# Linear attention plus a gated MLP on one core: scaling of q moved to ACT and POOL, states per unit, and the last three chunks transposed by DMA

## The chip, the cores and the metric

The kernel runs on one core of a Trainium2 chip. The metric is the device time of one execution in microseconds. A timed execution is about 2.1 us longer than the span from the first to the last instruction that a profile shows. The kernel before takes 250.9 to 251.2 us in its first timed runs.

Engine names: PE multiplies matrices, PEld is its weight load, DVE, ACT and POOL do elementwise work, SP issues most DMAs.

## The reference

Per batch and head, attention with a decay `lam` runs over blocks; its output, with the heads side by side, is the input `x` of a two-layer network.

```python
for b in range(nb):                       # blocks of the sequence
    intra = (qb @ kb.T * Dmask) @ vb      # inside the block, with decay
    inter = (qb * lam_pow) @ kv_state     # what earlier blocks left
    out[block] = intra + inter
    kv_state = lam_block * kv_state + (kb * rev_pow).T @ vb
h = x @ w_in                              # 3072 x 512 @ 512 x 2048
g = h * erf(softplus(h))
y = g @ w_out                             # 2048 x 512
```

Inputs are q, k, v of 4 x 8 x 768 x 64 in fp32; the result is 3072 x 512.

## The kernel before

The work is cut into 16 units (batch, half of the sequence, four heads) and 8 chunks of 384 tokens, two units each. A unit is loaded, q and k are scaled by powers of the decay (`scale_q`, `scale_k`), both are transposed (`alpha`), the scores are made (`beta`), then the states (`states`), then the attention output (`outputs`), which ACT copies into `xT`. A chunk then has 16 up-projection steps (`up_proj`), four gate steps, and 12 down-projection steps. The program is written out period by period: period `c` holds the up-projections of chunk `c`, the gates of chunk `c-1`, the down-projections of chunk `c-2` and, put in at numbered positions, the attention of the chunk that comes next.

```python
def scale_q(self):                                   # DVE
    ...
        nc.vector.tensor_scalar(out=self.qd[...], in0=qs[:, hh], scalar1=qpow[:, h:h + 1], ...)
def scale_k(self):                                   # POOL
    ...
        nc.gpsimd.tensor_scalar(out=self.kd[...], in0=ks[:, hh], scalar1=kpow[:, h:h + 1], ...)
def alpha(self):                                     # 12 PE transposes, 2 copies out of PSUM
    ps = pa.tile([128, 2, 8, 128], BF16, name="qk_ps", tag="a")
    ...
            nc.tensor.transpose(out=ps[:, pr, n, :], in_=self.qd[:, pr, n], identity=ident[:])
            nc.tensor.transpose(out=ps[:, pr, HB + n, :], in_=self.kd[:, pr, n], identity=ident[:])
...
def up_proj(c, ko):
    ...                                              # 4 matmuls of 384 columns into h_ps (2 buffers)
    nc.vector.tensor_copy(h[:, ko % GRP, :], ps[:, 0:T])
    if ko % GRP == GRP - 1:
        e = es[c, g] = mw.tile([128, GRP, T], FP32, name="e_sb", tag="e", bufs=5)
        nc.scalar.activation(out=e[:], in_=h[:], func=Af.Softplus)
def gate(c, g, dve=()):
    nc.scalar.activation(out=e[:], in_=e[:], func=Af.Erf)
    for j in range(GRP):                             # on POOL, in the last period on DVE
        eng.tensor_mul(gs[c][:, g * GRP + j, :], h[:, j, :], e[:, j, :])
def down_proj(c, i):                                 # 4 of 16 matmuls of 512 columns into y_ps (2 buffers)
    ...
    if part == 3:
        nc.scalar.copy(y[:], ps[:])                  # ACT, then a store by SP
...
for fn in pool:                                      # pool: k and v scaling, then the gates
    put(0, fn)
...
pts = {0: (8, 12, 10, 14, 15, 16), 1: (5, 11, 8, 13, 15, 16), ...}   # alpha, alpha, beta, beta, states, outputs
```

Of the kernel before, what the change touches and what calls it, by code (L numbers as in the profile page):

```python
# [12 lines left out]
BF16 = mybir.dt.bfloat16  # L13
# [7 lines left out]
def kernel(  # L21
# [19 lines left out]
    KI, KO = DM // 128, DF // 128  # L41
    GRP = 4
# [72 lines left out]
    load(1, "k", nc.scalar)  # L115
    load(1, "q")
# [19 lines left out]
    class Unit:  # L136
# [5 lines left out]
        def scale_q(self):  # L142
            qs = staged[self.i][0]
            self.qd = aw.tile([128, 2, HB, 2, D], BF16, name="qd", tag="qd", bufs=4)
            for hh in range(4):
                h = 4 * self.pp + hh
                nc.vector.tensor_scalar(out=self.qd[:, hh // 2, :, hh % 2, :], in0=qs[:, hh],  # L147
                                        scalar1=qpow[:, h:h + 1], scalar2=None, op0=Alu.mult)

        def scale_k(self):  # L150
            ks = staged[self.i][1]
            self.kd = aw.tile([128, 2, HB, 2, D], BF16, name="kd", tag="kd", bufs=4)
            for hh in range(4):
                h = 4 * self.pp + hh
                nc.gpsimd.tensor_scalar(out=self.kd[:, hh // 2, :, hh % 2, :], in0=ks[:, hh],  # L155
                                        scalar1=kpow[:, h:h + 1], scalar2=1.0,
                                        op0=Alu.mult, op1=Alu.mult)
# [12 lines left out]
        def alpha(self):  # L170

            ps = pa.tile([128, 2, 8, 128], BF16, name="qk_ps", tag="a")
            self.qk = aw.tile([128, 2, 2, HB, 128], BF16, name="qk_sb", tag="qk")
            for pr in range(2):
                for n in range(HB):
                    nc.tensor.transpose(out=ps[:, pr, n, :], in_=self.qd[:, pr, n], identity=ident[:])  # L176
                    nc.tensor.transpose(out=ps[:, pr, HB + n, :], in_=self.kd[:, pr, n], identity=ident[:])  # L177
            for pr in range(2):
                copy = nc.scalar.copy if self.i < 4 and pr else nc.vector.tensor_copy
                copy(self.qk[:, pr].rearrange("p a n i -> p (a n) i"), ps[:, pr, 0:2 * HB, :])  # L180

        def beta(self):

            self.sc = aw.tile([128, 2, 2, HB, 128], BF16, name="sc_sb", tag="sc")
            for pr in range(2):
                ps = pa.tile([128, 2, 4, 128], FP32, name="sc_ps", tag="a")
                for n in range(HB):
                    for hh in range(2):
                        r = slice(64 * hh, 64 * hh + 64)
                        nc.tensor.matmul(ps[:, hh, n, :], lhsT=self.qk[r, pr, 1, n, :],  # L190
                                         rhs=self.qk[r, pr, 0, n, :])
                h0 = 4 * self.pp + 2 * pr
                m = mask[:, h0:h0 + 2, :]
                m = bass.AP(tensor=m.tensor, offset=m.offset, ap=[m.ap[0], m.ap[1], [0, HB], m.ap[2]])
                nc.vector.tensor_mul(self.sc[:, pr], ps[:, :, 0:HB, :], m)  # L195
# [4 lines left out]
    def states(c):  # L200

        ps = pa.tile([128, 2, 8, D], FP32, name="dk_ps", tag="a")
        us = units[2 * c:2 * c + 2]
# [25 lines left out]
    def outputs(c):  # L229
# [4 lines left out]
        first = set()  # L234

        def start(*key):
            new = key not in first
            first.add(key)
            return new

        for u, ps in zip(us, pss):
            for n in range(HB):
# [3 lines left out]
                for pr, hh in ((0, 0), (1, 1), (1, 0), (0, 1)):  # L246
                    r = slice(64 * hh, 64 * hh + 64)
                    nc.tensor.matmul(ps[r, pr, n, :], lhsT=u.kv[r, pr, g, :], rhs=u.qk[r, pr, 0, n, :],  # L248
                                     start=start(u.pp, pr, hh), stop=False, skip_group_check=True)
        for u, ps in zip(us, pss):  # L250
            for pr in range(2):
                for n in range(HB):
                    for hh in range(2):
                        r = slice(64 * hh, 64 * hh + 64)
                        nc.tensor.matmul(ps[r, pr, n, :], lhsT=u.vb[:, pr, n, hh, :],  # L255
                                         rhs=u.sc[:, pr, hh, n, :],
                                         start=start(u.pp, pr, hh), stop=True, skip_group_check=True)
# [6 lines left out]
    def up_proj(c, ko):  # L264
# [10 lines left out]
        if c == 0 and ko % 2:  # L275
# [34 lines left out]
    def slots(c):  # L310

        a, b = units[2 * c:2 * c + 2]
        return [a.alpha, b.alpha, a.beta, b.beta, lambda: states(c), lambda: outputs(c)]

    a, b = units[0:2]
    a.scale_q()
    a.scale_k()
    a.alpha()
    late_consts()
    load(3)  # L320
    a.beta()
# [8 lines left out]
    b.alpha()  # L330
    b.beta()
    states(0)
# [9 lines left out]
    for c in range(NCH + 2):  # L342
# [23 lines left out]
        elif c == 1:  # L366
            pool = kv(u) + gates[:1] + kv(u + 1) + gates[1:2] + [lambda: [load_wout(g) for g in range(4)]] + gates[2:]
        elif c == 2:
            pool = gates[:2] + kv(u, u + 1) + gates[2:]
        elif c == 3:  # L370
            pool = kv(u, u + 1) + gates
            put(21, units[u + 2].scale_kv)
            put(25, units[u + 3].scale_kv)
# [4 lines left out]
        for pos, w in {0: ((6, u), (11, u + 1)), 1: ((3, u), (9, u + 1)), 2: ((15, u), (19, u + 1)),  # L378
                       3: ((3, u), (6, u + 1), (21, u + 2), (25, u + 3))}.get(
                           c, ((8, u + 2), (13, u + 3))):  # L380
            if w < len(units):
                put(pos, units[w].scale_q)
                put(pos, load, w + 3)
        if c + 1 < NCH:
            pts = {0: (8, 12, 10, 14, 15, 16), 1: (5, 11, 8, 13, 15, 16), 2: (17, 21, 19, 23, 25, 27),
# [39 lines left out]
```

## Time and profile before

| | us |
|---|---|
| timed, first runs | 250.91 (250.9 to 251.16) |
| span of the execution that was profiled first | 252.3 |
| up to the first matmul of the third chunk | 69.75 |
| from there to the first down-projection matmul | 14.34 |
| from there to the end | 168.21 |

The lines of the next block are from the table of stretches of the kernel before, with rows left out. Each has: stretch, its length, then busy time and number of instructions of PE, PEld, DVE, ACT and POOL, the granted tensor clock as a share of full speed, the busy share of the DMA engines, and GB/s.

```profile
0.00:69.00 69.00, 44.89 (x464) 26.39 (x465) 42.87 (x110) 33.82 (x36) 36.16 (x67) 1.00 0.91 178
69.00:84.00 15.00, 14.00 (x64) 7.03 (x64) 8.16 (x15) 13.91 (x12) 13.01 (x19) 0.78 0.96 175
...
105.00:130.00 25.00, 23.97 (x223) 13.91 (x226) 19.37 (x48) 17.30 (x16) 24.16 (x38) 1.00 0.73 172
130.00:219.00 89.00, 87.98 (x721) 49.23 (x731) 56.09 (x125) 62.21 (x55) 64.19 (x76) 1.00 0.20 60
```

Up to 69 us PE is busy for 44.89 us only, while DMA moves 178 GB/s. From 130 to 219 us PE is busy for 87.98 of 89 us. Between the two lies a stretch at a mean clock of 0.78. The view of who waited for whom, limited to PE and to 84 to 222 us, gives the sum, the number of waits and the longest:

```profile
PE h_ps L272 <- DVE h_sb L278: 1.3, 2, 0.8
```

So in that stretch PE is the limit, with 1.3 us of waits for another engine. The "restart" is the first up-projection matmul of the third chunk, after PE has stood idle. The chain of work that ended last shows what holds it at 69.75 us (start, duration, engine, tile, line):

```profile
61.39 2.24 POOL wout_sb L133 x3
63.62 3.88 POOL gT L290 x4
67.52 1.48 ACT e_sb L281
69.00 0.70 ACT xT L258
69.75 6.32 PE h_ps L272 x20
```

POOL's issue of the w_out loads and then its gates of the first chunk come first. A softplus on ACT (L281) waits for a gate to free its `e` buffer. The `xT` copy (L258) stands behind that softplus, and the up-projection needs it.

### The profile page before, as it was taken

How to read it: one execution, taken by the hardware profiler on the slowest of the kernel's cores; microseconds unless marked ns; L12 is line 12 of the kernel's file. 1: busy time of each engine (PE TensorE's matmuls, PEld its weight loads, DVE VectorE, ACT ScalarE, POOL GpSimd, SP SyncE). 2: the span in 40 equal slices, each digit the busy share in tenths (PEclk: the TensorE clock that was granted, in tenths of full speed). 3: DMA queues.
4: the chain of work that ended last, by engine and by line, in shares of the span. 5: the costliest groups of instructions: out<-in, count | busy, mean ns of one | idle time of the engine just before them, and what ended most of it. 6: DMA issues, size and time to landing. Idle time of an engine off the chain costs nothing.

```text
span 252.3 us, 4777 instructions
## 1 busy us (share of the span) xinstructions
PE 218.2 (86%) x1770; PEld 119.5 (47%) x1792; DVE 150.6 (60%) x350; ACT 146.6 (58%) x136; POOL 155.9 (62%) x225
## 2 busy tenths in 40 slices
PE   0347978888499999999899999999999999996993
PEld 0225444445245545555465556555655555542441
DVE  1655468499537873879669936993577344418300
ACT  4022475895299242794399249924993499569010
POOL 2275034099969996299999993991199219930000
PEclk9999999999959999999999999999999999999799
DMA  6979998777998377578577701020101010210212
GB/s 139 212 162 197 197 203 180 171 162 146 193 196 176 79 174 174 157 179 229 132 178 177 211 3 42 0 86 0 45 0 68 18 42 3 83 42 1 102 67 83
DMA packets 84647, 29.68 MB, mean 118 GB/s; under 512 B 77456, under 2 KB 81552, under 8 KB 84624
## 3 DMA queue, kind: packets, MB, share of 16 engines
q1 hardware_dynamic: 77200, 24.40, 39.9%
q0 software_dynamic: 4224, 4.19, 10.2%
q10 hardware_dynamic: 3200, 0.79, 1.5%
q8 instruction: 14, 0.23, 0.4%
q14 instruction: 9, 0.07, 0.1%
HBM read 27.27 MB, written 6.29 MB: 133 GB/s over the span
## 4 chain that ended last, share of the span: by engine, by line
PE 69%; DVE 13%; POOL 5%; DMA 4%; ACT 4%; issue 3%; SPq 1%; DVEq 0%; ACTq 0%; POOLq 0%
PE y_ps L301 31%; PE h_ps L272 28%; DVE h_sb L278 3%; POOL gT L290 3%; DVE qd L147 3%; DMA k_st<-in_k_dram 3%; DVE sc_sb L195 3%; DVE kv L225 2%; PE sc_ps L190 2%; PE o_ps L255 2%; PE o_ps L248 2%; PE qk_ps L176 2%; PE qk_ps L177 1%; ACT xT L258 1%; ACT e_sb L287 1%
## 5 line engine op out<-in xcount | busy, mean ns | idle before, releaser
L290 POOL TENSOR_TENSOR gT<-h_sb,e_sb 128x384 bf16<-128x384 f32 x112 | 107.9, 1011 | 38.6 <-ACT e_sb L287 31.5
L272 PE MATMUL h_ps<-xT,win_sb 128*128 128x384 bf16 x512 | 102.8, 336 | 7.9 <-DVE h_sb L278 4.3
L278 DVE COPY h_sb<-h_ps 128x384 f32<-128x384 f32 x120 | 65.4, 554 | 58.9 <-PE h_ps L272 50.6
L301 PE MATMUL y_ps<-wout_sb,gT 128*128 128x512 bf16 x362 | 92.1, 385 | 3.6 <-ACT y_sb L305 2.3
L272 PEld LDWEIGHTS <-win_sb 128*128 128x128 bf16 x512 | 49.6, 100 | 50.2 <-issue 16.5
L281 ACT ACTIVATE e_sb<-h_sb 128x1536 f32<-128x1536 f32 x32 | 47.3, 1483 | 33.9 <-DVE h_sb L278 20.8
L301 PEld LDWEIGHTS <-gT 128*128 128x128 bf16 x384 | 37.1, 99 | 40.9 <-issue 4.8
L287 ACT ACTIVATE e_sb<-e_sb 128x1536 f32<-128x1536 f32 x32 | 44.8, 1472 | 0.1
L155 POOL TENSOR_SCALAR kd<-k_st,pows 128x192 bf16<-128x192 f32 x64 | 26.5, 442 | 19.4 <-DMA k_st<-in_k_dram 15.3
L195 DVE TENSOR_TENSOR sc_sb<-sc_ps,mask 128x768 bf16<-128x768 f32 x32 | 29.2, 950 | 5.2 <-PE sc_ps L190 5.1
L305 ACT COPY y_sb<-y_ps 128x512 f32<-128x512 f32 x24 | 13.8, 577 | 28.7 <-PE y_ps L301 26.0
L176 PE MATMUL qk_ps<-ident,qd 128*128 128x128 bf16 x96 | 14.3, 231 | 9.7 <-DVE qd L147 9.2
L147 DVE TENSOR_SCALAR qd<-q_st,pows 128x192 bf16<-128x192 f32 x64 | 21.9, 404 | 1.1 <-ACT pows L101 1.0
L258 ACT CAST xT<-o_ps 128x768 bf16<-128x768 f32 x16 | 12.0, 800 | 17.9 <-PE o_ps L255 17.9
L163 POOL CAST vb<-v_st 128x384 bf16<-128x384 f32 x32 | 15.7, 522 | 8.1 <-DMA v_st<-in_v_dram 8.0
L180 DVE COPY qk_sb<-qk_ps 128x768 bf16<-128x768 bf16 x28 | 14.5, 552 | 8.9 <-PE qk_ps L177 8.4
L176 PEld LDWEIGHTS <-qd 128*128 128x128 bf16 x96 | 9.6, 102 | 12.9 <-DVE qd L147 11.9
L190 PE MATMUL sc_ps<-qk_sb 64*128 64x128 bf16 x192 | 9.5, 228 | 6.0 <-ACT qk_sb L180 4.7
L177 PE MATMUL qk_ps<-ident,kd 128*128 128x128 bf16 x96 | 14.1, 230 | 0.0
L225 DVE SCALAR_TENSOR_TENSOR kv<-kv,lamblk,dk_ps 128x64 bf16<-128x64 bf16 x64 | 12.9, 275 | 1.4 <-PE dk_ps L214 1.4
L190 PEld LDWEIGHTS <-qk_sb 64*128 64x128 bf16 x192 | 5.7, 97 | 12.2 <-ACT qk_sb L180 5.4
L248 PE MATMUL o_ps<-qk_sb,kv 64*64 64x128 bf16 x160 | 8.6, 229 | 2.5 <-DVE kv L225 1.9
(37 smaller groups left out, 88.1 us busy)
## 6 DMA issues: line engine op xcount, KB each, us to landing
q_st<-in_q_dram SPq DMA_DIRECT2D x64, 96.0 KB, 2.6
v_st<-in_v_dram SPq DMA_DIRECT2D x64, 96.0 KB, 2.6
out_dram<-y_sb SPq DMA_DIRECT2D x24, 256.0 KB, 2.0
k_st<-in_k_dram SPq DMA_DIRECT2D x56, 96.0 KB, 2.5
win_sb<-in_moe_w_in_dram POOLq DMA_DIRECT2D x4, 512.0 KB, 10.1
wout_sb<-in_moe_w_out_dram POOLq DMA_DIRECT2D x4, 512.0 KB, 10.5
k_st<-in_k_dram ACTq DMA_DIRECT2D x8, 96.0 KB, 3.6
lam_bc<-in_lam_dram SPq DMA_DIRECT2D x1, 4.0 KB, 2.8
```

The source lines that it names most:

```text
L147: nc.vector.tensor_scalar(out=self.qd[:, hh // 2, :, hh % 2, :], in0=qs[:, hh], scalar1=qpow[:, h:h + 1], scalar2=None, op0=Alu.mult)
L155: nc.gpsimd.tensor_scalar(out=self.kd[:, hh // 2, :, hh % 2, :], in0=ks[:, hh], scalar1=kpow[:, h:h + 1], scalar2=1.0, op0=Alu.mult, op1=A ...
L176: nc.tensor.transpose(out=ps[:, pr, n, :], in_=self.qd[:, pr, n], identity=ident[:])
L190: nc.tensor.matmul(ps[:, hh, n, :], lhsT=self.qk[r, pr, 1, n, :], rhs=self.qk[r, pr, 0, n, :])
L195: nc.vector.tensor_mul(self.sc[:, pr], ps[:, :, 0:HB, :], m)
L225: nc.vector.scalar_tensor_tensor(out=u.kv[:, pr, g + 1, :], in0=u.kv[:, pr, g, :], scalar=lamblk[:, hp:hp + 1], in1=dk, op0=Alu.mult, op1= ...
L272: nc.tensor.matmul(ps[:, 0:T], lhsT=win_sb[:, kc, ko * 128:(ko + 1) * 128], rhs=xT[:, kc, :], start=(kc == 0), stop=(kc == KI - 1))
L278: nc.vector.tensor_copy(h[:, ko % GRP, :], ps[:, 0:T])
L281: nc.scalar.activation(out=e[:], in_=h[:], func=Af.Softplus)
L287: nc.scalar.activation(out=e[:], in_=e[:], func=Af.Erf)
L290: eng.tensor_mul(gs[c][:, g * GRP + j, :], h[:, j, :], e[:, j, :])
L301: nc.tensor.matmul(ps[:], lhsT=gs[c][:, ko, t * 128:(t + 1) * 128], rhs=wout_sb[:, ko, :], start=(ko == 0), stop=(ko == KO - 1))
```

## The change

Its intent: take DVE off the critical start by scaling q of units 0 to 3 on ACT and of units 4 and 5 on POOL; make the states unit by unit; issue the intra part of the outputs before the inter part, which needs the states; and take 72 of the 192 transposes off PE by letting the DMA engines transpose the last six units. For units 10 and 11 the DMA needs k early, so their k scaling moves from POOL, where it came late, to DVE. All 12 DMA transposes stand in SP's queue. The diff below is shortened: square brackets stand for calls, and not shown are the new order of the first two units, the layout of the transposed tile, and the buffers of `qd` (3 for 4) and of that tile (3).

```diff
-    load(1, "k", nc.scalar)
-    load(1, "q")
+    load(1, "qk")
...
+                if self.i < 4:
+                    nc.scalar.mul(self.qd[...], qs[:, hh], qpow[:, h:h + 1])
+                elif self.i < 6:
+                    nc.gpsimd.tensor_scalar(out=self.qd[...], in0=qs[:, hh], ...)
+                else: ...                                     # DVE, as before
+                eng = nc.vector if self.i in (10, 11) else nc.gpsimd       # scale_k
...
+        def flip(self):                                      # FIRST_X = 10
+            if self.i < FIRST_X:
+                return
+            self.qk = aw.tile([128, 2, 2, HB, 128], BF16, name="qk_sb", tag="qk", bufs=3)
+            for a, src in enumerate((self.qd, self.kd)):
+                nc.sync.dma_start_transpose(self.qk[:, a]..., src[:]...)
...                                      # outputs: intra of both units first, then inter
-        if c == 0 and ko % 2:
+        if c == 0 and ko % 2 or c == 1 and ko in (9, 11, 13, 15):          # h copies on ACT
...
         elif c == 1:
-            pool = kv(u) + gates[:1] + kv(u + 1) + gates[1:2] + [w_out loads] + gates[2:]
+            pool = [x.scale_k, x.scale_q, x.cast_v, load, y.scale_k, y.scale_q, y.cast_v, load] + gates[:2]
+            pool += [w_out loads] + gates[2:]
...
         elif c == 3:
-            put(21, units[u + 2].scale_kv); put(25, units[u + 3].scale_kv)  # q at 21, 25 too
+            for w, pos in ((u + 2, 12), (u + 3, 17)):
+                put(pos, units[w].scale_k); put(pos, units[w].scale_q)
+                put(pos + 2, units[w].flip); put(pos + 3, units[w].cast_v); put(pos + 3, load, w + 3)
...
+        for w in (2 * c + 4, 2 * c + 5):
+            if c > 3 and w < len(units):
+                put(26, units[w].flip)
-        1: (5, 11, 8, 13, 15, 16)
+        1: (3, 9, 5, 11, 13, 16)
```

More of the change, by code (lines that the diff above doesn't have):

```diff
@@ L41 @@
     KI, KO = DM // 128, DF // 128
+    FIRST_X = 10
     GRP = 4
@@ L143, in scale_q @@
             qs = staged[self.i][0]
-            self.qd = aw.tile([128, 2, HB, 2, D], BF16, name="qd", tag="qd", bufs=4)
+            self.qd = aw.tile([128, 2, HB, 2, D], BF16, name="qd", tag="qd", bufs=3)
             for hh in range(4):
                 h = 4 * self.pp + hh
-                nc.vector.tensor_scalar(out=self.qd[:, hh // 2, :, hh % 2, :], in0=qs[:, hh],
-                                        scalar1=qpow[:, h:h + 1], scalar2=None, op0=Alu.mult)
+                if self.i < 4:
+                    nc.scalar.mul(self.qd[:, hh // 2, :, hh % 2, :], qs[:, hh], qpow[:, h:h + 1])
+                elif self.i < 6:
+                    nc.gpsimd.tensor_scalar(out=self.qd[:, hh // 2, :, hh % 2, :], in0=qs[:, hh],
+                                            scalar1=qpow[:, h:h + 1], scalar2=1.0,
+                                            op0=Alu.mult, op1=Alu.mult)
+                else:
+                    nc.vector.tensor_scalar(out=self.qd[:, hh // 2, :, hh % 2, :], in0=qs[:, hh],
+                                            scalar1=qpow[:, h:h + 1], scalar2=None, op0=Alu.mult)
         def scale_k(self):
@@ L154, in scale_k @@
                 h = 4 * self.pp + hh
-                nc.gpsimd.tensor_scalar(out=self.kd[:, hh // 2, :, hh % 2, :], in0=ks[:, hh],
-                                        scalar1=kpow[:, h:h + 1], scalar2=1.0,
-                                        op0=Alu.mult, op1=Alu.mult)
+                eng = nc.vector if self.i in (10, 11) else nc.gpsimd
+                eng.tensor_scalar(out=self.kd[:, hh // 2, :, hh % 2, :], in0=ks[:, hh],
+                                  scalar1=kpow[:, h:h + 1], scalar2=1.0,
+                                  op0=Alu.mult, op1=Alu.mult)
         def cast_v(self):
@@ L170, in alpha @@
         def alpha(self):
+            if self.i >= FIRST_X:
+                return
             ps = pa.tile([128, 2, 8, 128], BF16, name="qk_ps", tag="a")
-            self.qk = aw.tile([128, 2, 2, HB, 128], BF16, name="qk_sb", tag="qk")
-            for pr in range(2):
-                for n in range(HB):
-                    nc.tensor.transpose(out=ps[:, pr, n, :], in_=self.qd[:, pr, n], identity=ident[:])
-                    nc.tensor.transpose(out=ps[:, pr, HB + n, :], in_=self.kd[:, pr, n], identity=ident[:])
-            for pr in range(2):
-                copy = nc.scalar.copy if self.i < 4 and pr else nc.vector.tensor_copy
-                copy(self.qk[:, pr].rearrange("p a n i -> p (a n) i"), ps[:, pr, 0:2 * HB, :])
+            self.qk = aw.tile([128, 2, 2, HB, 128], BF16, name="qk_sb", tag="qk", bufs=3)
+            for a, src in enumerate((self.qd, self.kd)):
+                for pr in range(2):
+                    for n in range(HB):
+                        nc.tensor.transpose(out=ps[:, a, pr * HB + n, :], in_=src[:, pr, n], identity=ident[:])
+            for a in range(2):
+                copy = nc.scalar.copy if self.i < 4 and a else nc.vector.tensor_copy
+                copy(self.qk[:, a].rearrange("p r n i -> p (r n) i"), ps[:, a, 0:2 * HB, :])
+        def flip(self):
+            if self.i < FIRST_X:
+                return
+            self.qk = aw.tile([128, 2, 2, HB, 128], BF16, name="qk_sb", tag="qk", bufs=3)
+            for a, src in enumerate((self.qd, self.kd)):
+                nc.sync.dma_start_transpose(
+                    self.qk[:, a].rearrange("p r n i -> p (r n) i"),
+                    src[:].rearrange("p r n h d -> p (r n h d)"))
         def beta(self):
@@ L189, in beta @@
                         r = slice(64 * hh, 64 * hh + 64)
-                        nc.tensor.matmul(ps[:, hh, n, :], lhsT=self.qk[r, pr, 1, n, :],
-                                         rhs=self.qk[r, pr, 0, n, :])
+                        nc.tensor.matmul(ps[:, hh, n, :], lhsT=self.qk[r, 1, pr, n, :],
+                                         rhs=self.qk[r, 0, pr, n, :])
                 h0 = 4 * self.pp + 2 * pr
@@ L198, with states @@
     xTs = {}
-    def states(c):
+    def states(*us):
         ps = pa.tile([128, 2, 8, D], FP32, name="dk_ps", tag="a")
-        us = units[2 * c:2 * c + 2]
         nblk = HB if us[0].half == 0 else HB - 1
@@ L233, in outputs @@
         pss = [pa.tile([128, 2, 4, 128], FP32, name="o_ps", tag="a") for _ in us]
-        first = set()
-        def start(*key):
-            new = key not in first
-            first.add(key)
-            return new
+        for u, ps in zip(us, pss):
+            for pr in range(2):
+                for n in range(HB):
+                    for hh in range(2):
+                        r = slice(64 * hh, 64 * hh + 64)
+                        nc.tensor.matmul(ps[r, pr, n, :], lhsT=u.vb[:, pr, n, hh, :],
+                                         rhs=u.sc[:, pr, hh, n, :],
+                                         start=n == 0, stop=u.half * HB + n == 0, skip_group_check=True)
         for u, ps in zip(us, pss):
@@ L247, in outputs @@
                     r = slice(64 * hh, 64 * hh + 64)
-                    nc.tensor.matmul(ps[r, pr, n, :], lhsT=u.kv[r, pr, g, :], rhs=u.qk[r, pr, 0, n, :],
-                                     start=start(u.pp, pr, hh), stop=False, skip_group_check=True)
-        for u, ps in zip(us, pss):
-            for pr in range(2):
-                for n in range(HB):
-                    for hh in range(2):
-                        r = slice(64 * hh, 64 * hh + 64)
-                        nc.tensor.matmul(ps[r, pr, n, :], lhsT=u.vb[:, pr, n, hh, :],
-                                         rhs=u.sc[:, pr, hh, n, :],
-                                         start=start(u.pp, pr, hh), stop=True, skip_group_check=True)
+                    nc.tensor.matmul(ps[r, pr, n, :], lhsT=u.kv[r, pr, g, :], rhs=u.qk[r, 0, pr, n, :],
+                                     start=False, stop=True, skip_group_check=True)
             nc.scalar.copy(xT[:, 2 * u.pp:2 * u.pp + 2, :].rearrange("p a (n i) -> p a n i", i=128),
@@ L312, in slots @@
         a, b = units[2 * c:2 * c + 2]
-        return [a.alpha, b.alpha, a.beta, b.beta, lambda: states(c), lambda: outputs(c)]
+        return [a.alpha, b.alpha, a.beta, b.beta, lambda: states(a, b), lambda: outputs(c)]
     a, b = units[0:2]
+    late_consts()
     a.scale_q()
@@ L318 @@
     a.alpha()
-    late_consts()
+    a.beta()
     load(3)
-    a.beta()
     b.scale_q()
@@ L330 @@
     b.alpha()
+    states(a)
     b.beta()
-    states(0)
+    states(b)
     outputs(0)
@@ L366 @@
         elif c == 1:
-            pool = kv(u) + gates[:1] + kv(u + 1) + gates[1:2] + [lambda: [load_wout(g) for g in range(4)]] + gates[2:]
+            x, y = units[u:u + 2]
+            pool = [x.scale_k, x.scale_q, x.cast_v, lambda: load(u + 3), y.scale_k, y.scale_q, y.cast_v,
+                    lambda: load(u + 4)] + gates[:2]
+            pool += [lambda: [load_wout(g) for g in range(4)]] + gates[2:]
         elif c == 2:
@@ L371 @@
             pool = kv(u, u + 1) + gates
-            put(21, units[u + 2].scale_kv)
-            put(25, units[u + 3].scale_kv)
+            for w, pos in ((u + 2, 12), (u + 3, 17)):
+                put(pos, units[w].scale_k)
+                put(pos, units[w].scale_q)
+                put(pos + 2, units[w].flip)
+                put(pos + 3, units[w].cast_v)
+                put(pos + 3, load, w + 3)
         else:
@@ L377 @@
             put(0, fn)
-        for pos, w in {0: ((6, u), (11, u + 1)), 1: ((3, u), (9, u + 1)), 2: ((15, u), (19, u + 1)),
-                       3: ((3, u), (6, u + 1), (21, u + 2), (25, u + 3))}.get(
+        for pos, w in {0: ((6, u), (11, u + 1)), 1: (), 2: ((15, u), (19, u + 1)),
+                       3: ((3, u), (6, u + 1))}.get(
                            c, ((8, u + 2), (13, u + 3))):
@@ L383 @@
                 put(pos, load, w + 3)
+        for w in (2 * c + 4, 2 * c + 5):
+            if c > 3 and w < len(units):
+                put(26, units[w].flip)
         if c + 1 < NCH:
-            pts = {0: (8, 12, 10, 14, 15, 16), 1: (5, 11, 8, 13, 15, 16), 2: (17, 21, 19, 23, 25, 27),
+            pts = {0: (8, 12, 10, 14, 15, 16), 1: (3, 9, 5, 11, 13, 16), 2: (17, 21, 19, 23, 25, 27),
                    3: (8, 10, 13, 17, 21, 25)}.get(c, (3, 6, 11, 15, 19, 24))
```

## The prediction

> **What bounds the kernel now** (table of stretches, chain of waits).
> - 0 to 69.75 us: not PE, busy 44.9 us. DMA moves 170 to 190 GB/s, SP issues loads nearly without pause (0.51 us each). The chain runs through k and v loads, ACT, then from 57.7 to 67.5 us POOL (gates of the first chunk, 3.9 us per group, 3.1 us of w_out issue), one softplus that waits for a gate to free its e buffer, and the next xT copy queued on ACT behind it. PE idles 2.37 us and restarts at a mean clock of 0.72 from 70 to 80 us.
> - 84 to 222 us: PE, which waits only about 1.5 us (view of who waits for whom), clock 1.00. Work taken off PE here is saved outright; off DVE, ACT or POOL it is not.
> - 222 to 252 us: tail, untouched.
>
> **What changes.**
> 1. Units 10 to 15 are transposed by DMA. 72 PE transposes go; warm, 12 take 0.67 us, so 6 x 0.67 = 4.0 us, all in the PE-bound stage. 12 PSUM copies leave DVE, off the path. Added: 12 DMA transposes of 192 KB on SP. No trace here times one. [...] From the 2.0 us landing of a 256 KB store I estimate 2.5 to 4 us each. Issued at position 26 of a 28-step period (about 25.9 us), two per unit, they have about 10 us before the first scores matmul of the next chunk and 14 us before the second: enough up to 3.5 us each in series.
> 2. First 25 us: q scaling leaves DVE (1.6 us per unit); unit 1's k load leaves ACT, whose issues held a copy until 12.65 us and PE for 3.9 us. The first up-projection (24.77 us) comes about 2 us earlier, held by loads and w_in.
> 3. But the restart at 69.75 us counts. POOL now does kd, qd and vb of units 4 and 5 before any gate, so the first gate waits for the last v of unit 5 (about 51 us, load-paced; before: 50.37, erf-paced). Then vb 1.0, two gates 7.8, issue 3.1, gate 3.9: 15.8 us, then softplus and copy. I expect the restart at 68 to 70 us, a gain of 0 to 2 us from all of the early part, with a longer PE idle (4 to 6 us), cold again.
> 4. Intra before inter hides the kv chain (PE waits of 0.8 us near 121, 0.4 near 171 us): about -1 us. Against it, kd and qd of units 10 and 11 run back to back on DVE (3.3 us) in the fourth period, ahead of h copies that PE needs: +0.5 to +1 us.
>
> **Sum.** -4.0 (transposes) -1.4 (start) -0.2 (order, DVE) = -5.6: 250.9 becomes 245.3 us, range 241.5 to 249.5. Chances: faster by over 2% 0.55, within 2% 0.39, slower 0.06.
>
> **What would show it.** (1) 120 PE transposes instead of 192; periods from 130 to 220 us each 1.3 us shorter; no PE wait on the DMA into qk_sb. (2) First up-projection at 22 to 23 us. (3) First 64-matmul run at 68 to 70 us, after a softplus waiting for a POOL gate and a longer PE idle. (4) No PE wait on kv after 84 us; some on h copies near 110 to 120 us.
>
> **What would make it wrong.** DMA transposes of over 5 us each, or slowed by loads and stores on their queue: PE would wait 3 to 10 us in each of the last three chunks. SP blocked by a transpose waiting for its buffer, holding loads. Or the early chain really loosening, so that PE restarts warm: another 3 to 5 us gained.

## More of the kernel before

Last, the tail, in the timeline of PE (start, duration, instructions, in brackets the idle time before and what ended it):

```profile
232.56 15.66 PE L301 MATMUL y_ps<-wout_sb,gT 128*128 128x512 bf16 x63 [2.33 <-ACT y_sb L305]
```

PE idles 2.33 us for a `y` copy that ACT does only after four Erfs.

## The result, and the profile after

The changed kernel took 251.63 us (250.96 to 251.86, four executions), the kernel before 251.03 us beside it. The ratio was 1.0019, with a 95% interval of 0.9999 to 1.0039. Ratios here are the mean time of one kernel's fast runs over that of the other's of the same rounds, so not quite the ratio of the medians quoted. A later session gave 250.84 us and 0.9973 (0.9922 to 1.0024). So the change is worth nothing that a timing shows, where 5.6 us were expected. The kernel before was faster here (251.03 us) than its own first profile (a span of 252.3 us, timed at 254.3 us), on which the prediction was built; the experiments begin there. In later sessions, on three chips, executions of the kernel before range from 250.4 to 254.1 us.

The table of stretches of the changed kernel:

```profile
0.00:69.00 69.00, 44.20 (x464) 27.04 (x465) 34.10 (x82) 41.80 (x56) 40.78 (x76) 0.98 0.91 179
69.00:84.00 15.00, 14.19 (x70) 7.19 (x70) 9.63 (x20) 13.32 (x11) 13.01 (x19) 0.89 0.93 173
...
105.00:130.00 25.00, 22.21 (x195) 12.39 (x198) 19.47 (x50) 14.60 (x15) 21.23 (x31) 1.00 0.78 174
130.00:219.00 89.00, 87.93 (x678) 47.56 (x689) 52.58 (x117) 63.15 (x55) 66.13 (x76) 1.00 0.34 84
```

From 130 to 219 us PE is as full as before. From 105 to 130 us PE is busy for 22.21 us instead of 23.97. The waits of PE from its first down-projection to the tail (82.6 to 219 us):

```profile
PE h_ps L284 <- DVE h_sb L290: 2.2, 4, 0.8
PE dk_ps L233 <- DVE sc_sb L215: 0.7, 1, 0.7
PE qk_ps L187 <- DVE qd L154: 0.3, 1, 0.3
```

PE's waits there rose from 1.3 us (the kernel before) to 3.2 us; none of them is for a DMA transpose. A transpose of 192 KB took a median of 3.2 us to land (2.7 to 4.8), a load of 96 KB by SP 2.5 to 2.6 us, a store of 256 KB 2.0 us, and SP spent 1.2 to 2.3 us on each transpose. Two of them in SP's queue:

```profile
148.43 2.32 SPq L198 DMA_TRANSPOSE qk_sb<-qd  x1
150.84 1.24 SPq L198 DMA_TRANSPOSE qk_sb<-kd  x1
```

The start, in the timeline of POOL:

```profile
49.96 1.63 POOL L150 TENSOR_SCALAR qd<-q_st,pows 128x192 bf16<-128x192 f32 x4
51.54 0.95 POOL L171 CAST vb<-v_st 128x384 bf16<-128x384 f32 x2
52.45 7.70 POOL L302 TENSOR_TENSOR gT<-h_sb,e_sb 128x384 bf16<-128x384 f32 x8
60.09 3.06 POOL L133 DMA_DIRECT2D wout_sb<-in_moe_w_out_dram  x4
```

in the timeline of ACT:

```profile
67.05 1.48 ACT L293 ACTIVATE e_sb<-h_sb 128x1536 f32<-128x1536 f32 x1 [2.72 <-POOL gT L302]
68.44 1.48 ACT L270 CAST xT<-o_ps 128x768 bf16<-128x768 f32 x2
```

and in that of PE:

```profile
69.28 13.50 PE L284 MATMUL h_ps<-xT,win_sb 128*128 128x384 bf16 x64 [4.10 <-ACT xT L270]
```

The first up-projection started at 20.92 us instead of 24.77. The third chunk's nevertheless starts at 69.28 us, within half a microsecond of before: the gates start after the v of unit 5, at 52.45 us, and the same softplus stands in front of the same copy.

The tail, in PE's timeline:

```profile
229.33 15.66 PE L313 MATMUL y_ps<-wout_sb,gT 128*128 128x512 bf16 x63 [2.33 <-ACT y_sb L317]
```

### The profile page after: what moved, and what is told of

It reads as the page before. It is cut to its first block, busy times and chain, and to the rows that moved or that the text cites. A ratio compares the mean times of both kernels' runs of the same rounds, so it can differ in the third digit from the quotient of the medians.

```text
span 248.8 us, 4643 instructions
## 1 busy us (share of the span) xinstructions
PE 212.8 (86%) x1698; PEld 115.9 (47%) x1720; DVE 138.1 (56%) x318; ACT 153.7 (62%) x156; POOL 157.0 (63%) x225
## 4 chain that ended last, share of the span: by engine, by line
PE 57%; POOL 12%; DVE 8%; DMA 6%; issue 6%; SPq 5%; ACT 4%; POOLq 0%; ACTq 0%; DVEq 0%
PE y_ps L313 29%; PE h_ps L284 20%; POOL gT L302 8%; SPq L67 5%; DMA k_st<-in_k_dram 4%; PE o_ps L258 2%; DVE h_sb L290 2%; PE sc_ps L210 2%; POOL kd L163 2%; DVE sc_sb L215 2%; DVE kv L244 2%; ACT e_sb L299 2%; PE o_ps L268 2%; PE qk_ps L187 1%; POOL qd L150 1%
## 5 line engine op out<-in xcount | busy, mean ns | idle before, releaser
L290 DVE COPY h_sb<-h_ps 128x384 f32<-128x384 f32 x116 | 63.3, 554 | 69.7 <-PE h_ps L284 56.3
L163 POOL TENSOR_SCALAR kd<-k_st,pows 128x192 bf16<-128x192 f32 x56 | 23.9, 440 | 24.2 <-DMA k_st<-in_k_dram 20.0
L187 PE MATMUL qk_ps<-ident,qd 128*128 128x128 bf16 x60 | 6.1, 237 | 9.2 <-ACT qd L148 8.2
L154 DVE TENSOR_SCALAR qd<-q_st,pows 128x192 bf16<-128x192 f32 x40 | 13.6, 402 | 0.0
L190 DVE COPY qk_sb<-qk_ps 128x768 bf16<-128x768 bf16 x16 | 8.4, 553 | 8.0 <-PE qk_ps L187 8.0
L210 PE MATMUL sc_ps<-qk_sb 64*128 64x128 bf16 x192 | 8.8, 229 | 3.3 <-ACT qk_sb L190 2.3
L288 ACT COPY h_sb<-h_ps 128x384 f32<-128x384 f32 x12 | 5.7, 474 | 8.8 <-PE h_ps L284 8.8
L302 DVE TENSOR_TENSOR gT<-h_sb,e_sb 128x384 bf16<-128x384 f32 x16 | 7.6, 554 | 4.9 <-ACT e_sb L299 4.9
```

The source lines that it names most:

```text
L163: eng.tensor_scalar(out=self.kd[:, hh // 2, :, hh % 2, :], in0=ks[:, hh], scalar1=kpow[:, h:h + 1], scalar2=1.0, op0=Alu.mult, op1=Alu.mult)
L210: nc.tensor.matmul(ps[:, hh, n, :], lhsT=self.qk[r, 1, pr, n, :], rhs=self.qk[r, 0, pr, n, :])
```

## The experiments

An edit "of the tail" and others recur, so the kernels are grouped by question.

### Which execution of the kernel before is the one to compare with?

**before_again**: no edit, a second profile.

> The unchanged kernel before, profiled once more. Its first profile had a span of 252.3 us, while its timed runs of 250.9 to 251.2 us correspond to spans of about 249 us, so the profiled execution was some 3 us longer than the ones that are timed. Theory A (the first profile caught an execution that differs in one stage, and the change was compared with a picture 3 us too slow): the span is now 248.5 to 249.5 us, with the 3 us gone from one stage, most likely the restart near 70 us where the tensor clock was 0.72. Theory B (the profiler itself costs this kernel 3 us): the span is again about 252 us while its timed runs stay at 251 us. Ratio 1.00 in both.

250.76 us, span 248.9 us instead of 252.3. Theory A holds, but not in one stage. PE's timeline of the tail in this second profile:

```profile
230.86 13.97 PE L301 MATMUL y_ps<-wout_sb,gT 128*128 128x512 bf16 x63 [2.33 <-ACT y_sb L305]
```

The same 63 matmuls after the same 2.33 us of idle took 13.97 us here and 15.66 us in the first profile. From the restart to the first down-projection it was 13.03 us against 14.34. The two differences make 3.0 of the 3.4 us. The granted clock explains them. Cut finer, the table of stretches shows it at half speed in the first profile's tail and near its restart, and in before_again near the restart alone:

```profile
68.80:75.50 6.70, 5.75 (x18) 2.56 (x18) 2.06 (x4) 6.67 (x7) 4.71 (x6) 0.50 1.22 197
232.70:236.00 3.30, 3.30 (x9) 1.15 (x8) 2.85 (x7) 0.30 (x1) 0.00 (x0) 0.50 0.42 159
```

```profile
65.50:72.20 6.70, 4.90 (x41) 2.99 (x42) 1.29 (x5) 5.04 (x5) 5.39 (x6) 0.50 1.22 196
```

Near the restart the half clock lasted 6.83 us in the first profile, by the clock record of its trace, and about 6.8 us in before_again, by its mean clocks (0.92 from 47 to 69 us, 0.89 from 69 to 84 us, 1.00 in the stretches beside them). In before_again it came about 3.3 us earlier (65.5 against 68.8 us), so that part of it fell on PE's idle and on the attention matmuls before, and less on the up-projections. These are the stretches of 226 to 233 us, first in before_again, then in the changed kernel, whose tail was the long one:

```profile
226.00:233.00 7.00, 4.61 (x21) 2.04 (x21) 6.75 (x15) 5.30 (x6) 0.00 (x0) 1.00 0.20 73
```

```profile
226.00:233.00 7.00, 4.62 (x14) 1.77 (x14) 6.31 (x14) 3.76 (x5) 0.00 (x0) 0.76 0.20 75
```

The mean clock was 1.00 or 0.76. The missing 0.24 of 7 us is 1.7 us, the difference of the tails. Over all kernels with this idle of 2.33 us, nine traces in all, five had the long tail (15.66 us) and four the short one (13.97 us); one of the five is a slow run. The clock agrees: from 222 us to the end its mean is 0.91 to 0.95 in the five and 0.97 to 1.00 in the four. The clock records of the first profile and of the changed kernel show one stretch at 0.50 in each of their tails, of 3.41 us (from 232.61 and from 229.70 us). The same instructions after the same idle can do either. 3.41 us at a clock of 0.50 cost 1.7 us (15.66 less 13.97). In these two records every stretch at 0.50 that ends before the last matmul is 3.41 us or 6.83 us long, and the stretches at 1.00 between them are multiples of 3.41 us too (157.01 us is 46 of them). Why the clock fell in one execution and not in another, no trace here shows.

For the comparison this means that the first profile of the kernel before, on which the prediction was built, had the half clock both in its tail and over most of its restart, while its timed runs (250.9 to 251.2 us) match the execution with the short tail. The traced execution of the changed kernel had the long one.

**after_again**: the changed kernel, no edit, six executions.

> The changed kernel as it is, more executions. Theory A (its four executions at 251.0 to 251.9 us had a cold clock in the tail by chance; a warm tail is 1.7 us shorter): times in two groups, about 249.3 to 250.2 and 251 to 252 us, and a mean 0.5 to 1.5 us below the kernel before on the same chip. Rival B (251.6 us is its time): all executions within 251 to 252 us, ratio 1.00 or above.

Four executions of 250.4 to 251.0 us and two of 252.0 and 252.9 us; ratio 0.9973. The traced one, 252.86 us, had the long tail and from restart to first down-projection 13.93 us. There are two groups, but about 0.7 us higher than theory A had them, and the mean is only 0.7 us below the kernel before, with an interval that includes none. That the clock makes this spread is shown for the traced execution alone: the mean clocks do not sort the two groups (0.973 to 0.986 in the faster one, 0.977 in both of the slower). The change's own worth is small.

### The two halves of the change, one at a time

**transposes_only**: the kernel before with the DMA transposes of units 10 to 15, all issued at position 26.

```diff
+        for w in (2 * c + 4, 2 * c + 5):
+            if c > 2 and w < len(units):
+                put(26, units[w].flip)
```

> The kernel before with the DMA transposes alone: units 10 to 15 flipped at position 26 of each period, qk with 3 buffers and qd with 3, all of the early part and the fourth period as before. Theory A (72 PE transposes are 4.0 us of the PE-bound stage, and they are saved in full): 4 us faster, 247 us, ratio 0.984. Rival B (the transposes save less, because DMA, SP or a buffer wait gives it back): 0 to 2 us faster, with PE waits on the DMA into qk_sb or with h or y waits after 130 us.

253.65 us against 253.21 for the kernel before in that session: no gain. The cause is a flaw of this version that teaches something. The queue of SP, and then PE, at the start of its fifth period:

```profile
131.48 2.02 SPq L67 DMA_DIRECT2D v_st<-in_v_dram  x4
133.60 1.31 SPq L177 DMA_TRANSPOSE qk_sb<-qd  x1
134.96 1.28 SPq L177 DMA_TRANSPOSE qk_sb<-kd  x1
```

```profile
137.83 0.82 PE L203 MATMUL sc_ps<-qk_sb 64*128 64x128 bf16 x12 [3.75 <-DMA qk_sb<-kd]
```

The scores matmul waited 3.75 us for the transposed k. In this version k of units 10 and 11 is scaled on POOL at the end of the fourth period; it is ready at 122.5 and 125.1 us, but the transposes stand on SP behind loads, the last twelve of them issued from 126.77 us on, so they start at 133.60 us. Behind the wait four up-projection matmuls take 1.06 us where four took 0.81 us in front of it, and the mean clock from 130 to 155 us is 0.93, which would be 3.5 us at 0.50 (an estimate from that mean): up to another 1.7 us. So 3.75 and up to 1.7 us of loss stand against the 4.0 us saved; from the first down-projection to the end, both with the short tail, the traces give 167.47 us against 166.51 in before_again. The change avoids this in two ways at once: it scales that k on DVE, earlier, and issues these two units' transposes at positions 14 and 19, ahead of the loads. Whether moving the transposes alone would do, no run tests.

**before_x12_tail**: DMA transposes of units 12 to 15 only, whose data are ready in time, with the tail edit explained below; its yardstick is **before_tail_again** in the same session.

```diff
+    FIRST_X = 12
```

> The kernel before with the tail edit and DMA transposes of units 12 to 15 alone, whose scaled q and k are ready some 10 us before they are needed. Theory A (48 PE transposes at 0.056 us save 2.7 us in the PE-bound stage): 2.2 to 3 us faster than the yardstick, 245.3 to 247 us, no PE wait on a transpose. Rival B (the saving is lost again behind the transposes): under 1 us faster.

> The kernel before with the tail edit once more, as the yardstick of the other runs here. 248 to 249.4 us, as it was.

246.87 us against 248.54 us; the ratios to the kernel before are 0.9792 and 0.9868, so 0.8% apart, with intervals that just overlap; the 1.7 us between the medians are less than the 2.2 to 3 us of theory A. In the traces the stretch from the first down-projection to the end shrank from 163.98 to 161.32 us, by 2.66 us; 48 transposes at 0.056 us are 2.7 us. So theory A's saving is there, whole, in that stretch. Of it 1.6 us are lost again before: this execution restarted 0.6 us later and took 14.46 against 13.53 us up to the first down-projection. The mean clocks of the two traces (0.986 over 245.3 us, 0.993 over 246.4 us) make it about 6.9 us at half clock against 3.4, none of it in the last matmuls, which take 21.75 us in both; that the difference lies at the restart is an estimate. A second pair agrees: x12_tail and early_tail (both below) differ by the same 48 transposes alone, and the stretch takes 161.47 against 164.17 us, 2.70 us less. So with the data ready the DMA transposes replaced the PE transposes at full value here (2.66 and 2.70 of 2.7 us).

**early_only** and **early_tail**: the early part of the change alone (all transposes on PE, fourth period as before), the second with the tail edit.

```diff
-    FIRST_X = 10
+    FIRST_X = 16
-                eng = nc.vector if self.i in (10, 11) else nc.gpsimd
+                eng = nc.gpsimd
...                # period 3 as in the kernel before: positions 21 and 25
```

> The changed kernel with all transposes on PE again and its fourth period as in the kernel before; what is left of the change is its early part, the states per unit and intra before inter. Theory A (the early part costs time against an ordinary run of before, since POOL does q of units 4 and 5 and a cold PE restarts after 4 us of idle): 2 to 4 us slower than before, 253 to 255 us. Rival B (the early part is neutral and the loss lies in the fourth period): within 1 us of before, 250 to 252 us.

> The early part of the change alone, with the tail edit. Theory A (the first up-projection 3 us earlier, but the restart near 70 us still held by POOL's gates, which now stand behind q, k and v of two units: no gain, or a loss of up to 1 us): 248.5 to 250.3 us, 0 to 1 us slower than the yardstick. Rival B (the early part gains the 1.4 us that was predicted): 246.5 to 248 us.

early_only: 252.27 us, ratio 0.9981 (0.9923 to 1.0039) in a session where the kernel before wandered from 250.9 to 254.1. The loss of 2 to 4 us of its theory A is not there; the ratio is that of rival B, though the time lies 0.3 us above its range. early_tail: 249.91 us, 1.4 us slower than before_tail_again (ratios 0.9915 and 0.9868, intervals that overlap). Rival B of early_tail (a gain of 1.4 us) is out. Reading one milestone in every trace of a fast run with the xT copies where they were and no filler: the first down-projection came at 82.4 to 84.3 us in six traces of kernels with the old early part (mean 83.4), and at 82.6 to 84.5 us in six with the new one (mean 83.7). Each group spreads over 2 us, so the 0.3 us between them cannot be told from none. The new early part gains 3 to 4 us at the first up-projection and none at the first down-projection.

**p4_as_before**: the changed kernel with its fourth period put back and all six units transposed at position 26.

> The changed kernel with only its fourth period put back: kd and v of units 10 and 11 on POOL at positions 21 and 25, q on DVE there, flips of both at position 26. The changed kernel showed 2.5 us of PE waits between 111 and 122 us on DVE (h copies, scores) in that period. Theory A (kd on DVE in that period costs 1.5 to 2.5 us): 249.3 to 250 us, 1.5 to 2.5 us faster than the changed kernel. Rival B (the waits only move): within 0.5 us of the changed kernel, 251.2 to 252 us.

254.96 us, but three of its four executions, the profiled one among them, were slow, so this run decides nothing; the one fast execution took 250.94 us. It also has the flaw of transposes_only: its trace shows a PE wait of 3.3 us for the transposed k.

**x12_tail** asks the same question without that flaw: the changed kernel, fourth period as before, transposes from unit 12 on, tail edit.

> The changed kernel with its fourth period as in the kernel before (kd of units 10 and 11 on POOL, late), DMA transposes only for units 12 to 15, whose data are ready in time, and the tail edit. It keeps 48 of the 72 saved PE transposes (2.7 us) and drops the DVE work that cost PE 1.7 us of waits between 111 and 122 us. Theory A (both sizes are right): 0.3 to 1 us faster than the changed kernel with the tail edit, no PE wait over 0.9 us between 105 and 125 us, no PE wait on a DMA transpose at all. Rival B (transposes of units 12 and 13 come late too, or the DVE waits return elsewhere): slower than it by 0.5 us or more.

247.43 us; ratio 0.9778 against 0.9798 for the changed kernel with the tail edit (after_tail), 0.2% or 0.5 us faster, the size of theory A, though the intervals overlap. It gives up 24 saved transposes (1.3 us) and is still not slower; its stretch from the first down-projection to the end is 161.47 us against 162.06 in after_tail. The only PE wait above 0.2 us between 105 and 125 us is one of 0.82 us, as in the kernel before.

The fourth period of the changed kernel shows what it gives up instead. DVE:

```profile
114.10 1.36 DVE L163 TENSOR_SCALAR kd<-k_st,pows 128x192 bf16<-128x192 f32 x4
115.38 1.36 DVE L154 TENSOR_SCALAR qd<-q_st,pows 128x192 bf16<-128x192 f32 x4
116.66 1.81 DVE L215 TENSOR_TENSOR sc_sb<-sc_ps,mask 128x768 bf16<-128x768 f32 x2
118.39 1.01 DVE L290 COPY h_sb<-h_ps 128x384 f32<-128x384 f32 x2
```

PE in the changed kernel, then in before_again:

```profile
111.57 0.81 PE L284 MATMUL h_ps<-xT,win_sb 128*128 128x384 bf16 x4 [0.38 <-DVE h_sb L290]
...
117.66 0.57 PE L233 MATMUL dk_ps<-vb,kd 128*64 128x64 bf16 x24 [0.70 <-DVE sc_sb L215]
118.99 1.46 PE L284 MATMUL h_ps<-xT,win_sb 128*128 128x384 bf16 x8 [0.76 <-DVE h_sb L290]
...
121.97 0.81 PE L284 MATMUL h_ps<-xT,win_sb 128*128 128x384 bf16 x4 [0.66 <-DVE h_sb L290]
```

```profile
119.48 0.81 PE L272 MATMUL h_ps<-xT,win_sb 128*128 128x384 bf16 x4 [0.82 <-DVE h_sb L278]
```

DVE has k and q of a unit in one block, 2.7 us, and the score work of 1.8 us (a multiplication by the decay mask) behind it; PE waits for h copies and scores, 2.50 us in sum against 0.82 us.

### The tail

**before_tail** and **after_tail**: the gates of the last-but-one period spread, so that the y copies do not stand behind all four Erfs on ACT.

```diff
-        for fn in pool:
-            put(0, fn)
+        for j, fn in enumerate(pool):
+            put((0, 4, 4, 8)[j] if c == NCH else 0, fn)
```

> The kernel before with one edit in its last-but-one period: the four gate steps, all issued at its start, are issued at positions 0, 4, 4 and 8, so that the y copies on ACT stand between the Erfs and not behind all four. In every trace PE idles 2.33 us there for a y copy, and the 63 matmuls after it took 13.97 us in some executions and 15.66 us in others, with a granted clock of 1.00 or 0.94 in the tail. Theory A (the idle and the clock drop it triggers cost 2.3 us always and 1.7 us more in some executions): span 2 to 4 us shorter, 247 to 249 us timed, tail clock 1.00, and less spread between runs. Rival B (the wait only moves to the gates on DVE): within 0.7 us of before.

> The changed kernel with the same edit of the tail. Theory A (the change is 1.5 us ahead of the kernel before when the tail starts, as the traces show, and lost that in the tail by a cold clock that its executions happened to get): about 1.5 us (1 to 2.5) faster than the kernel before with the same tail edit, 3 to 4 us faster than before, 246.5 to 248 us. Rival B (the change is worth nothing at any point): the same time as the kernel before with the tail edit, within 0.5 us.

before_tail: 248.96 us, ratio 0.9833 (0.9782 to 0.9883). after_tail: 247.88 us, ratio 0.9798 (0.9747 to 0.9848). ACT and PE in before_tail:

```profile
225.71 1.48 ACT L287 ACTIVATE e_sb<-e_sb 128x1536 f32<-128x1536 f32 x1
227.09 0.57 ACT L305 COPY y_sb<-y_ps 128x512 f32<-128x512 f32 x1
227.56 2.86 ACT L287 ACTIVATE e_sb<-e_sb 128x1536 f32<-128x1536 f32 x2
```

```profile
221.56 21.75 PE L301 MATMUL y_ps<-wout_sb,gT 128*128 128x512 bf16 x98
```

The y copy now stands between two Erfs, and 98 matmuls run in one piece of 21.75 us, without idle. In all nine traces with this edit these last matmuls (98, or 100 in three traces) take the same 21.75 us; four such matmuls take 0.86 us at a clock of 1.00 (the kernel before, 130 to 219 us), so 100 take 21.5 and a half clock of 3.41 us does not fit. Of the nine without it, five take 15.66 us for 13.97. With both kernels freed of it, the changed one is 0.4% or 1.1 us ahead in the medians, with intervals that overlap. That is at the lower end of what theory A of after_tail expected. In the traces its stretch from first down-projection to end is 162.06 us against 164.04, 2.0 us less; the rest is the restart.

### The restart near 70 us

**after_filler**: 18 useless matmuls where PE idles before the restart, to keep its clock up.

```diff
+            if c == 1:
+                put(16, keep_warm, 18)     # matmuls into a PSUM tile that nothing reads
```

> The changed kernel with 18 extra 512-column matmuls into a PSUM buffer that nothing reads, placed behind the third chunk's outputs, where PE otherwise idles 4 to 5 us before the restart at 69.3 us. They add no useful work. Theory A (the idle makes the granted clock drop, and the run of 64 matmuls after it pays for that: 13.2 to 14.6 us against 10.4 us at 162 ns each): restart still at 69 to 70 us, the run of 64 takes 10.4 to 11.8 us, and the kernel is 1.5 to 3.5 us faster than the changed one, 248 to 250 us. Rival B (that run is slow for other reasons, such as h copies on DVE): the run still takes 13 us or more, same time or slower.

249.74 us, ratio to the kernel before 0.9953 (0.989 to 1.0017). PE:

```profile
65.66 3.83 PE L325 MATMUL warm_ps<-win_sb 128*128 128x512 bf16 x17 [0.16 <-issue]
...
70.32 11.71 PE L284 MATMUL h_ps<-xT,win_sb 128*128 128x384 bf16 x62 [0.22 <-ACT xT L270]
```

From the restart to the first down-projection it took 12.24 us instead of 13.33, and 62 matmuls 11.71 us where the changed kernel took 13.50 us for 64. From 69.3 to 72.6 us the clock is 0.50 in the changed kernel, and 11 matmuls take these 3.30 us; here the first 25 of the 62 take 4.86 us. So in this stretch the idle did cost clock. The time is 1.9 us below the changed kernel's first median, which is theory A's size, but only 1.1 us below that of after_again, in other sessions, and the interval just reaches no gain over the kernel before. Its tail was the long one.

**after_xt_first**: the third chunk's outputs one position earlier, so that its xT copies stand before the softplus.

```diff
-            1: (3, 9, 5, 11, 13, 16)
+            1: (3, 9, 5, 11, 13, 15)
```

> The changed kernel with the third chunk's outputs one step earlier (position 15 for 16 in the second period), so that on ACT its xT copies stand before the softplus that waits for a POOL gate; nothing else. Theory A (that softplus is what holds PE's restart at 69.3 us and buries the 3 us that the early part gained): restart at 62 to 65 us instead of 69.3, PE idle before it under 2 us, the run of 64 up-projection matmuls slowed by h buffers waiting for gates, in all 2 to 4 us faster than the changed kernel. Rival B (the restart is held by something else, such as kv or the h copies): restart within 1.5 us of 69.3 and the time within 0.7 us of the changed kernel.

247.76 us, ratio 0.9813 (0.976 to 0.9866). PE:

```profile
65.42 1.22 PE L284 MATMUL h_ps<-xT,win_sb 128*128 128x384 bf16 x6
66.86 11.71 PE L284 MATMUL h_ps<-xT,win_sb 128*128 128x384 bf16 x62 [0.22 <-ACT xT L270]
```

The third chunk starts at 65.42 us instead of 69.28, so the softplus was what held it. The first down-projection comes at 78.41 instead of 82.61 us, 4.2 us earlier. But PE then waits where it did not wait before. The waits from 78 to 100 us:

```profile
PE qk_ps L187 <- POOL kd L163: 1.3, 2, 0.8
PE y_ps L313 <- ACT y_sb L317: 1.1, 1, 1.1
```

About 2.4 of the 4.2 us are returned there: POOL's k and ACT's y copy now come late. This execution had the short tail, so part of its lead over the changed kernel is clock. A cleaner pair is x12_tail and combo (below), which differ by this position alone and both take 21.75 us for the last 98 matmuls: 247.43 and 244.07 us, in two sessions. In their traces the first down-projection comes 7.1 us earlier, and 3.0 us of it are returned. Part of the 7.1 us may be clock: by the mean clocks x12_tail (0.985 over 245.7 us) had about 7.4 us at half clock and combo (0.993 over 241.6 us) about 3.4; where they lie was not shown.

**before_xt_tail**: the same two edits on the kernel before.

> The kernel before with two edits and nothing of the change: the tail's gates spread, and the third chunk's outputs at position 15 of the second period, so that its xT copies stand before the softplus that waits for a gate. Theory A (the restart near 69.3 us is held by that softplus in the kernel before too): restart at 66 to 68 us with less PE idle before it, 1.5 to 3.5 us faster than the kernel before with the tail edit alone, 245.5 to 247.5 us. Rival B (in the kernel before, DVE and the kv chain hold the outputs as late as the softplus does): restart at 68.5 us or later and under 0.7 us of gain over the tail edit alone.

249.07 us, ratio 0.9902, no better than the tail edit alone (248.96 and 248.54 us in other sessions). Its first down-projection is at 80.84 us, but from there to the end it takes 166.46 us against 164.0 us; the same two waits, for POOL's k (1.2 us) and for ACT's y copy (1.0 us), are among what returned it. Rival B's time, for a different reason: the restart did come earlier, at 67.71 us, and all was given back. In the kernel before the edit gains nothing that these sessions show. With the new early part it pays (x12_tail to combo); that this is because the outputs are ready earlier there is argued from the restart (63.37 us in combo, 67.71 us here), not tested.

### The corrections together

**combo**: the changed kernel with the tail edit, xT first, fourth period as before, transposes from unit 12 on. **combo_kd_act**: the changed kernel with the tail edit, xT first, all 72 transposes by DMA, and k of units 10 and 11 scaled on ACT.

```diff
+                if self.i in (10, 11):
+                    nc.scalar.mul(self.kd[...], ks[:, hh], kpow[:, h:h + 1])
+                    continue
```

> The changed kernel with the tail edit, xT ahead of the softplus, its fourth period as in the kernel before and DMA transposes for units 12 to 15 only. Theory A (the three corrections act in different stages and add up: tail 3.5 us, restart 2.5 to 3 us, fourth period 0.5 us): 244 to 245.5 us, some 2.5 to 3.2 percent faster than the kernel before. Rival B (time gained at the restart is given back later): 246.5 us or more.

> The changed kernel with the tail edit and xT ahead of the softplus, all 72 transposes by DMA, and kd of units 10 and 11 on ACT instead of DVE. Theory A (the 1.7 us of PE waits in the fourth period come from 3.3 us of kd on DVE in front of h copies and scores): the waits of 0.7 us near 117 to 121 us shrink to below 0.9 us in sum, and it is 0.5 to 1.5 us faster than the version with transposes of four units only, 243 to 244.5 us. Rival B (ACT, in order behind a softplus that waits for a gate, holds kd and with it the transposes and SP): PE waits on ACT or on the DMA into qk_sb between 110 and 140 us, and 245 us or more.

combo: 244.07 us, ratio 0.9704 (0.9659 to 0.9749), as its theory A had it. combo_kd_act: 242.62 us (242.2 to 243.2), ratio 0.9651 (0.9609 to 0.9694), correct, 1.45 us below combo (theory A: 0.5 to 1.5), and faster than both kernels. All of PE's waits in it from 105 to 130 us:

```profile
PE h_ps L287 <- DVE h_sb L293: 0.4, 1, 0.4
```

Of the 2.5 us of waits of the fourth period 0.4 are left. after_xt_first, which up to there differs only in having that k on DVE, still has all 2.5 us, so they did come from the k scaling on DVE. The mean granted clock of the traced execution is shown as 1.00, and the six executions lie within 1.0 us.

## Why the prediction was wrong

- **Step 1, the transposes: -4.0 us. Right in size, where they are.** There are 72 PE matmuls fewer. Two periods of the PE-bound stage, from the wait of 0.82 us at 119.48 to that of 0.44 us at 169.27 us in before_again, take 49.79 us; the same two points in the changed kernel are 121.97 and 169.07, 47.10 us, so 1.35 us less per period (1.3 predicted). No PE wait on a transpose; they landed in 2.7 to 4.8 us, median 3.2 (2.5 to 4 estimated). The prediction has all of them at position 26; units 10 and 11 are at 14 and 19.
- **Step 2, the first 25 us. Right in kind.** The first up-projection came 3.9 us earlier than in the first profile and about 3 us earlier than in before_again, more than the 2 us predicted.
- **Step 3, the start: -1.4 us. This term failed: it measured about +0.3 us, within the spread nothing.** The path stood as predicted: the gates come after the last v of unit 5, the restart is at 69.28 us behind the softplus, and PE idled 4.1 to 5.0 us before it. What was mis-sized is the first gate: 52.45 us and not about 51. It is not held by the load of v, as predicted, since POOL does not idle before that v; POOL gets the last of unit 5's k at 48.76 us and then needs 3.7 us for the rest of k, for q and for v, and 1.6 us of that is the q that the change gave it. SP issues this k from 45.56 us on, before the change from 45.15, so the loads were not earlier either. after_xt_first shows that the softplus was the hold, and that lifting it needs further corrections to keep the gain.
- **Step 4, order and DVE: -0.2 us. This term failed most: it measured +1.9 us (3.2 us of PE waits from the first down-projection to the tail, against 1.3).** Two things were wrong in it. The gain of 1 us for intra before inter was read off the wrong wait: the 0.8 and 0.4 us of PE idle near 121 and 171 us are waits for h copies on DVE, as the view of waits says, not for the states, and both are still there (0.66 us at 121.97 and 0.44 us at 169.07 us). DVE reached the first of these copies only after q and state work of its own (115.55 to 118.88 us in before_again), and issuing the intra part first does not change that. And k and q in one block on DVE cost 1.7 us of PE waits (2.50 against 0.82) plus 0.25 us for a q near 84 us, not 0.5 to 1 us.
- **The sum.** -4.0 + 0.3 + 1.9 is -1.8 us at equal clock. From first down-projection to end, both with the long tail, the traces give 166.19 against 168.21 us, -2.0. What was left, the tail's clock can hide: 1.7 us more or less by execution. The prediction named the tail as untouched and did not see that the profile it rested on had the half clock in the tail and over the restart, although its span plus 2.1 us did not fit the timed runs. Restart and tail made two executions of the kernel before differ by 3.0 us, 1.2% of the span, enough to hide the change.
- Of its reasons to be wrong, none came true: no transpose took over 5 us, PE did not wait for a load after 84 us, and PE did not restart warm (clock 0.50 from 69.3 to 72.6 us).

That the other three of the first four executions of the changed kernel had the long tail too is argued from their mean clock (0.976 to 0.979, as the traced one), not shown, and weakly: in after_again executions with that mean clock took 250.6 to 252.9 us. So is the share of luck in its first ratio.

## What to carry to other kernels

Work taken off the limiting engine is saved only if the work that makes room for it does not land in front of what that engine waits for: here 4.0 us of transposes were saved and 1.9 us lost to waits on DVE, nearly all behind a block of scaling, while the k scaling on ACT left 0.4 us of waits in that period. Look in each engine's order of instructions for one that waits on a slow partner and stands in front of a copy that the limiting engine needs (here the softplus at 67.05 us, the copy behind it at 68.44 us); moving it by one position, on top of the rebalanced start, gained what the rebalancing alone did not. Before comparing two kernels by a few microseconds, check that the span of each profile fits the timed runs, and remove idle gaps of the tensor engine first: here the tail's matmuls took 15.66 us for 13.97 behind the idle of 2.33 us in five of nine traces, with a mean clock of 0.91 to 0.95 from 222 us on, and once the idle was gone they took the same 21.75 us in all nine.
